# An FFT filter and MLP kernel: last FFT stage channel-major, residual by identity matmul, one-batch first units, loads paced

## The chip, the cores and the metric

The kernel runs on one core of one Trainium2 chip. The metric is the device time of one execution in microseconds (us). Before the change it was 720.28 us, the median of 3 runs (719.31 to 722.85). A run is "slow" when it is over 1.5% above the fastest of the same kernel. A "span" is the length of one profiled execution; it is about 2 us shorter than the device time.

Engines are called by the profile's names: PE is TensorE (matmul), PEld its weight loads, DVE VectorE, ACT ScalarE, POOL GpSimd and SP SyncE. "POOL queue" and "SP queue" mean the DMA transfers that those engines issue, in program order.

## The reference

```python
# x (8, 3136, 256); filt (1569, 256) complex; U (3136, 32); V (32, 3136)
X = np.fft.rfft(x, axis=1)
y = np.fft.irfft(X * F, n=3136, axis=1)          # a filter per channel
u = y + (y.transpose(0,2,1) @ U @ V).transpose(0,2,1)   # low-rank token mixing
out = u + np.maximum(u @ w_ch1, 0) @ w_ch2       # MLP 256 -> 1024 -> 256
```

## The kernel before

The length 3136 is split as 64 x 49. Batches are worked in units of two. For each unit:

1. **Stage 1 (`f1`)** multiplies x by a 64-point DFT and stores the result to DRAM (`ct1`), to be reloaded with another partition layout (`a2`).
2. **Middle stage (`mid`)**: for each of 33 frequencies a 49-point DFT (`pz`), the product with the filter on VectorE (`uv`), the inverse 49-point DFT (`pe`), an eviction on ScalarE, and a store to DRAM (`ct2`).
3. **Reload** (`load_e2`), then the low-rank product (`low_rank`, 25 multiplies that sum over all tokens).
4. **Groups** of 512 tokens: `stage4` (last FFT stage plus the low-rank term) makes u; transposes make it channel-major; `mm1` and `mm2` are the MLP.

The MLP of unit n fills TensorE while the middle stage of unit n+1 and stage 1 of unit n+2 are dealt out between its steps (8 steps per group) by a plan. Only the first unit has no MLP to hide behind.

```python
UNITS = [[0, 1], [2, 3], [4, 5], [6, 7]]

def f1(u):
    for c in range(6):
        asb = sb.tile([128, 4, bd], F16, tag="asb", bufs=2)
        for half in range(2):
            pf = ps.tile([128, 2, 512], F32, tag="w", bufs=1, name="pf")
            for i in range(nb):
                for h in range(2):
                    nc.tensor.matmul(pf[64*h:64*h+64, i, :], wf1[64*i:64*i+64, :],
                                     u.x[c][64*i:64*i+64, h, 2*half:2*half+2, :], ...)
            # evict: VectorE for one half, ScalarE for the other
            yield
        for h in range(2):
            nc.gpsimd.dma_start(dram(u.ct1, ...), asb[64*h:64*h+64])   # POOL queue
# ... cut

def stage4(gr):
    # four 64x64 multiplies by s2 (columns: two halves of the array), then
    # four with vsb as weights and u.h1 (low-rank result) streamed: u token-major
    gr.u16 = sb.tile([128, 2, 512], F16, tag="u", bufs=4, name="u16")
    nc.scalar.copy(gr.u16, pu)

def transposes(gr):
    # eight 128x128 transposes of u16 into pt (fp16), then
    nc.vector.tensor_copy(gr.ut[:, :, 0:gr.ntok], pt[:, :, 0:gr.ntok])

# end of mm2: nc.vector.tensor_add(dst, gv, uv)     adds u16 as the residual

# start
drain(f1(units[0])); load_x(units[1]); u_hat()
m0, fa = mid(units[0]), f1(units[1])
for i in range(34):                       # middle stage of unit 0, stage 1 of unit 1
    next(m0, None)
    if i >= 10 and i % 2 == 0:
        next(fa, None)
load_e2(units[0]); low_rank(units[0]); stage4(groups[0]); stage4(groups[1]); ...
# plan, per unit of `steps` steps (104 for 13 groups):
gens.append((mid(units[u.n + 1]), 34, 0, steps - 32))
gens.append((f1(units[u.n + 2]), 13, 0, steps))
# reload at step steps-31, low-rank product at steps-18, stage4 two groups ahead
```

## Time and profile before

| reading | value | view |
|---|---|---|
| first MLP multiply | 217.0 us | timeline |
| from there to the end | 500 us of a 717 us span | timeline |
| one 512-token group, late | 8.3 us | timeline |
| middle stage, first unit, per frequency | 2.1 to 2.2 us | timeline |

First, the page's rows of busy tenths. The span is cut into 40 slices of 17.9 us, a digit is the busy share of that slice in tenths, and PEclk is the granted clock.

```profile
PE   0000126766789999998999999999999999999996
DVE  0001125655553356621566654246665512122221
PEclk9999999999999999999999999999999999999999
DMA  9996567777673354578646351953343184230233
```

There are two regimes: TensorE has next to nothing to do in the first four slices and is full from the thirteenth on. In the first three the DMA engines are full. Next, the view of busy time by stretch: the window, its length, then busy us and instruction count of PE, PEld, DVE, ACT and POOL, then granted clock, DMA share and GB/s.

```profile
60.00:80.00 20.00, 2.76 (x20) 0.67 (x20) 3.67 (x3) 4.26 (x5) 4.99 (x8) 1.00 0.53 106
160.00:200.00 40.00, 28.57 (x64) 10.55 (x63) 22.66 (x20) 10.53 (x18) 11.19 (x17) 1.00 0.73 164
240.00:280.00 40.00, 39.84 (x278) 23.66 (x277) 20.67 (x22) 28.34 (x47) 8.42 (x13) 1.00 0.53 133
640.00:680.00 40.00, 40.00 (x301) 25.74 (x299) 9.68 (x14) 27.52 (x44) 0.00 (x0) 1.00 0.23 62
```

From 60 to 80 us every engine is busy for a quarter of the time at most and DMA for half: that stretch waits on latency. From 160 to 200 us PE shows 28.6 of 40, but with only 64 instructions. The view of waits says what the early stretch waits for (total us, times, longest):

```profile
DVE asb L224 <- DMA ct_0<-asb: 72.0, 5, 42.9
```

A stage-1 eviction needs its staging tile back. There are two such tiles, and U lies in one of them until stage 1 is over, so every tile waits for the store of the one before it. The first store was ready at 20.4 us (end of its eviction), but the POOL queue issued it at 50.15, behind the filter and weight loads: that wait took 42.9 us. The other four, 7.3 us each, are the plain round trip of a store; 72 us in five waits. In the middle stage the timeline (start, duration, engine, line, operation; in brackets the idle time before it and what ended it) shows a chain:

```profile
160.27 0.58 ACT L266 CAST esb<-pe 98x512 f16<-98x512 f32 x1 [1.52 <-PE pe L257]
160.90 0.59 PE L279 MATMUL pz<-a_384,tf_87 98*98 98x512 f16 x1 [0.67 <-ACT esb L266]
161.28 1.06 PE L257 MATMUL pe<-uv,g_89 98*98 98x512 f16 x2
161.53 1.22 DVE L286 TENSOR_TENSOR uv<-pz,fab 98x1024 f16<-98x1024 f32 x1 [0.89 <-PE pz L279]
162.42 0.58 ACT L266 CAST esb<-pe 98x512 f16<-98x512 f32 x1 [1.57 <-PE pe L257]
163.06 0.58 PE L279 MATMUL pz<-a_384,tf_87 98*98 98x512 f16 x1 [0.72 <-ACT esb L266]
```

`pz` and `pe` take turns in two PSUM buffers, so every next `pz` waits for ScalarE's eviction of `pe`: 163.06 − 160.90 = 2.16 us per frequency. Last, TensorE's timeline in a late group:

```profile
660.46 0.61 PE L371 MATMUL pt<-idn,u_6273 128*128 128x128 f16 x8
...
665.33 0.41 PE L350 MATMUL pu<-e_5383,s_91 64*64 64x512 f16 x4
665.68 0.61 PE L356 MATMUL pu<-h_5575,vsb 128*128 128x512 f16 x2
...
668.76 0.61 PE L371 MATMUL pt<-idn,u_6369 128*128 128x128 f16 x8
```

The transposes repeat after 668.76 − 660.46 = 8.30 us, and TensorE never waits between. The eight take 0.45 us (0.056 us from one start to the next). The four 64 x 64 multiplies of stage 4 take 0.35 us to the next multiply's start. Four of 512 columns one after the other would take 4 x 0.216 us. That is the overlap of small multiplies on different rows and columns of the array which the Trainium skill describes ("TensorE: Matmul & The Clock Gate", Part 3); this trace agrees.

### The profile page before, as it was taken

What the parts mean: (1) busy time and instruction counts of PE and PEld (TensorE: products, weight loads), DVE (VectorE), ACT (ScalarE), POOL (GpSimd) and SP (SyncE); (2) the same over time, 40 slices, a digit from 0 to 9 for tenths busy, and PEclk for the clock granted to TensorE, in tenths of its full rate; (3) what the DMA queues carried; (4) which work ended last, traced back from release to release, by engine and by line L of the source; (5) the groups of instructions that cost most, each with busy time, mean ns of one, the idle gap of its engine ahead of it and who ended that gap; (6) DMA issues with size and microseconds to landing.
All of it is one profiled execution on the core that took longest, in us unless ns stands there. A gap on an engine that the chain in (4) does not pass through costs nothing.

```text
span 716.9 us, 9884 instructions
## 1 busy us (share of the span) xinstructions
PE 581.4 (81%) x3797; PEld 330.4 (46%) x3797; DVE 288.1 (40%) x311; ACT 383.7 (54%) x634; POOL 126.8 (18%) x197
## 2 busy tenths in 40 slices
PE   0000126766789999998999999999999999999996
PEld 0000002222225656654565555565666665566664
DVE  0001125655553356621566654246665512122221
ACT  0004112432237676765767677567677765766663
POOL 3541342334111121211111111001111100000000
PEclk9999999999999999999999999999999999999999
DMA  9996567777673354578646351953343184230233
GB/s 189 172 181 137 117 130 213 189 166 155 158 203 71 82 150 131 132 193 218 190 119 196 88 150 44 283 162 115 103 126 108 54 183 129 63 88 15 76 89 95
DMA packets 47086, 97.88 MB, mean 137 GB/s; under 512 B 9336, under 2 KB 18108, under 8 KB 46942
## 3 DMA queue, kind: packets, MB, share of 16 engines
q0 software_dynamic: 27056, 43.93, 30.0%
q1 hardware_dynamic: 19984, 53.34, 27.3%
q8 instruction: 29, 0.48, 0.3%
q14 instruction: 17, 0.14, 0.1%
HBM read 64.05 MB, written 51.38 MB: 161 GB/s over the span
## 4 chain that ended last, share of the span: by engine, by line
PE 70%; DMA 13%; ACT 6%; issue 5%; POOL 2%; DVE 2%; SPq 1%; ACTq 0%; DVEq 0%; POOLq 0%
PE phh L379 22%; PE pc L415 21%; PE pe L257 10%; PE pz L279 5%; DMA ct_0<-asb 3%; PE pu L356 3%; PE pt L371 3%; ACT esb L266 3%; DMA x_75<-in_x_dram 3%; PE pu L350 2%; DMA fab<-in_filt_r_dram 2%; PE pf L214 2%; DMA e_2022<-ct_1 2%; ACT asb L222 2%; DMA fab<-in_filt_i_dram 2%
## 5 line engine op out<-in xcount | busy, mean ns | idle before, releaser
L379 PE MATMUL phh<-ut,w1sb 128*128 128x512 f16 (+1 forms) x832 | 237.6, 367 | 1.4 <-ACT h_2242 L382 0.2
L286 DVE TENSOR_TENSOR uv<-pz,fab 98x1024 f16<-98x1024 f32 x132 | 160.8, 1222 | 91.5 <-PE pz L279 91.2
L266 ACT CAST esb<-pe 98x512 f16<-98x512 f32 x128 | 74.6, 586 | 104.3 <-PE pe L257 103.3
L257 PE MATMUL pe<-uv,g_89 98*98 98x512 f16 x264 | 98.0, 462 | 3.0 <-DVE uv L286 2.0
L379 PEld LDWEIGHTS <-w1sb 128*128 128x128 f16 x832 | 78.6, 98 | 39.8 <-issue 12.6
L224 DVE CAST asb<-pf 128x1024 f16<-128x1024 f32 x24 | 29.3, 1222 | 97.0 <-DMA ct_0<-asb 72.0
L257 PEld LDWEIGHTS <-g_89 98*98 98x98 f16 x264 | 37.2, 144 | 54.3 <-issue 45.6
L214 PEld LDWEIGHTS <-wf_64 64*64 64x64 f16 x192 | 7.0, 114 | 118.8 <-issue 112.8
L222 ACT CAST asb<-pf 128x1024 f16<-128x1024 f32 x24 | 24.3, 1013 | 62.2 <-PE pf L214 60.5
L373 DVE COPY ut<-pt 128x1024 f16<-128x1024 f16 (+1 forms) x52 | 34.2, 657 | 15.2 <-PE pt L371 12.7
L214 PE MATMUL pf<-x_69,wf_64 64*64 64x512 f16 x8 | 1.3, 619 | 42.8 <-DVE asb L224 41.7
L279 PEld LDWEIGHTS <-tf_87 98*98 98x98 f16 x132 | 19.6, 148 | 17.3 <-issue 15.4
L268 POOL DMA_DIRECT2D ct_3<-esb x16 | 11.4, 710 | 90.2 <-ACT esb L266 83.6
L185 ACT COPY vsb<-vnat 128x768 f16<-128x768 f16 x4 | 7.0, 1829 | 34.6 <-DMA vnat<-in_moe_V_dram 34.6
L268 POOL DMA_DIRECT2D ct_1<-esb x16 | 11.5, 721 | 74.6 <-ACT esb L266 69.0
L268 POOL DMA_DIRECT2D ct_2<-esb x16 | 11.5, 720 | 63.5 <-ACT esb L266 50.4
L268 POOL DMA_DIRECT2D ct_0<-esb x16 | 11.9, 744 | 39.1 <-ACT esb L266 39.1
L214 PE MATMUL pf<-x_66,wf_64 64*64 64x512 f16 x8 | 1.9, 612 | 17.4 <-DMA x_66<-in_x_dram 16.1
L350 PEld LDWEIGHTS <-s_91 64*64 64x64 f16 x192 | 6.5, 103 | 19.4 <-issue 18.8
L227 POOL DMA_DIRECT2D ct_3<-asb x12 | 7.7, 648 | 27.2 <-ACT asb L222 27.2
L356 PEld LDWEIGHTS <-vsb 128*128 128x128 f16 x96 | 5.8, 97 | 11.1 <-issue 10.8
L227 POOL DMA_DIRECT2D ct_1<-asb x12 | 7.6, 640 | 12.5 <-ACT asb L222 12.5
(1605 smaller groups left out, 1235.7 us busy)
## 6 DMA issues: line engine op xcount, KB each, us to landing
out_dram<-och SPq DMA_DIRECT2D x128, 192.0 KB
ct_0<-esb POOLq DMA_DIRECT2D x16, 196.0 KB, 3.2
ct_1<-esb POOLq DMA_DIRECT2D x16, 196.0 KB, 3.5
ct_2<-esb POOLq DMA_DIRECT2D x16, 196.0 KB, 2.8
ct_3<-esb POOLq DMA_DIRECT2D x16, 196.0 KB, 2.8
ct_0<-asb POOLq DMA_DIRECT2D x12, 256.0 KB, 4.4
ct_1<-asb POOLq DMA_DIRECT2D x12, 256.0 KB, 4.2
ct_2<-asb POOLq DMA_DIRECT2D x12, 256.0 KB, 5.6
```

The costliest lines, as they stand in the source:

```text
L214: nc.tensor.matmul(pf[64 * h:64 * h + 64, i, :], wf1[64 * i:64 * i + 64, :], u.x[c][64 * i:64 * i + 64, h, 2 * half:2 * half + 2, :], star ...
L222: nc.scalar.copy(dst, src)
L224: nc.vector.tensor_copy(dst, src)
L257: nc.tensor.matmul(pe[0:98, 0:bd], g3[:, (2 * k + l) * 98:(2 * k + l + 1) * 98], uv[:, l * bd:(l + 1) * bd], start=(k != 32 and l == 0), s ...
L266: nc.scalar.copy(st["esb"][:, slot % 2, :], pe[0:98, 0:bd])
L268: nc.gpsimd.dma_start(dram(u.ct2, (slot - 1) * 98 * bd, [[bd, 98], [98 * bd, 2], [1, bd]]), st["esb"])
L279: nc.tensor.matmul(pz[0:98, 0:bd], tf2[:, k * 98:(k + 1) * 98], a2[slot // 4][:, slot % 4, :], start=True, stop=True)
L286: nc.vector.tensor_mul(uv.rearrange("p (f b d) -> p f b d", f=2, b=nb), zin, fin)
L356: nc.tensor.matmul(pu[:, h, jj * bd:(jj + 1) * bd], vsb[:, v0:v0 + 128], u.h1, start=False, stop=True, skip_group_check=True)
L373: nc.vector.tensor_copy(gr.ut[:, :, 0:gr.ntok], pt[:, :, 0:gr.ntok])
L379: nc.tensor.matmul(ph[:, 0:n], w1sb[:, dh * 1024 + t * 128:dh * 1024 + (t + 1) * 128], gr.ut[:, dh, 0:n], start=(dh == 0), stop=(dh == 1))
L415: nc.tensor.matmul(gr.pc[:, col * DM:(col + 1) * DM], gr.h[tt][:, i * 128:(i + 1) * 128], w2sb[:, tt * DM:(tt + 1) * DM], start=(tt == 0), ...
```

## The change

Its intent: make u channel-major directly in the last FFT stage, by using the reloaded tile as weights and `s2` as the moving operand. The transposes and one ScalarE cast go; the residual u is then added inside PSUM by an identity multiply. Stage 1 becomes one block-diagonal multiply over 128 rows. The first two units have one batch each, so that the MLP can start earlier; the filters are read once and mirrored in SBUF, the first unit's stage-1 stores go to the SP queue, U leaves stage 1's staging tiles, and x is loaded two tiles ahead.

```diff
-UNITS = [[0, 1], [2, 3], [4, 5], [6, 7]]
+UNITS = [[0], [1], [2, 3], [4, 5], [6, 7]]
 # wf1 and s2 become block-diagonal 128x128 (cut)
 # filters: loaded once into fab[:, 0], in two parts, then mirrored (cut)
+    def mirror_filters(a, z):
+        nc.sync.dma_start(fab[0:NR, 1, a:z, :], fab[NR:98, 0, a:z, :])
+        nc.sync.dma_start(fab[NR:98, 1, a:z, :], fab[0:NR, 0, a:z, :])
 # f1
+        eng = nc.sync if u.n == 0 else nc.gpsimd
+            if load_ahead and c + load_ahead <= nx:
+                load_x(u, c + load_ahead)
+                    nc.tensor.matmul(pf[:, i, :], wf1, u.x[c][:, r:r + 2, :], ...)
 # stage4: e2 and h1 as weights, s2 and vsb streamed
+            for i in range(4):
+                nc.tensor.matmul(pu[:, dh, i * 128:(i + 1) * 128],
+                                 e2[:, y, j % cj + jj, d0:d0 + 128], s2, ...)
+                nc.tensor.matmul(po[:, b], u.h1[:, d0:d0 + 128], vv[...], ...)
-        gr.u16 = sb.tile([128, 2, 512], F16, tag="u", bufs=4, name="u16")
-        nc.scalar.copy(gr.u16, pu)
-    def transposes(gr): ...
+        nc.vector.tensor_copy(gr.ut, pu)
 # residual, at the end of mm2
+                nc.tensor.matmul(o[:, dh*128:dh*128+128], gr.ut[:, dh, t0:t0 + n], idn,
+                                 start=False, stop=(dh == 1), skip_group_check=True)
-            nc.vector.tensor_add(dst, gv, uv)
+            nc.vector.tensor_copy(dst, gr.pc.rearrange(...))
 # plan over all 53 groups; first[n] is the first step of unit n
+    mids = [mid(units[0], "o")] + [mid(u) for u in units[1:]]
+    deal(f1s[1], 7, 0, 6)
+    deal(mids[1], 34, 9, 35)
+    for u in units[2:]:
+        z = first[u.n] - 22
+        a = first[u.n - 1]
+        if u.n == 2:
+            deal(f1s[2], 13, 14, a + 8)
+            deal(mids[2], 34, a + 10, z)
+        else:
+            deal(f1s[u.n], 13, first[u.n - 2] + 28, a - 4)
+            deal(mids[u.n], 34, a, z)
-                stage4(groups[n + 2])
+                stage4(groups[n + 1])
-                if step == 8 * (u.ng + 1) - 31:
+                if step == first[u.n + 1] - 20:
                     load_e2(units[u.n + 1])
-                if step == 8 * (u.ng + 1) - 18:
+                if step == first[u.n + 1] - 10:
                     low_rank(units[u.n + 1])
```

The middle stage of the next unit now ends 22 steps before that unit instead of 32, its reload is issued at −20 instead of −31, and its low-rank product comes at −10 instead of −18. A late step is about 1.04 us (8.3 us in 8 steps).

## The prediction

> **What bounds it now.** Two regimes. By the busy-time-by-stretch view TensorE is 93 to 100% busy in every stretch from 200 to 680 us; the first MLP multiply starts at 217.0 us (timeline). Before that, latency and DMA bind: TensorE works 5.3 of the first 80 us. First-stage stores sit on the GpSimd queue behind all loads (one eviction waits 42.9 us), then stage 1 goes at a store round trip (8.5 us) per tile until 98 us; the middle stage runs 111 to 212 us at 2.13 us per frequency, chained pz, pe, ScalarE eviction, next pz. There 512-column matmuls start 0.43 us apart, later 0.22: the half-rate clock that the Trainium skill ("TensorE: Matmul & The Clock Gate", Part 1) gives for a sparse array. The trace agrees, though the granted-clock row says 1.0.
>
> **Saturated part.** One 512-token group takes 8.3 us (timeline at 660 us): mm1 3.46, mm2 3.49, stage 4 0.88, transposes 0.45.
> - Removed: 8 transposes (56 ns each); a ScalarE cast (1.01 us); the fp16 eviction 0.69.
> - Added: 8 identity multiplies with weight loads, 0.45 us; VectorE evicts u from fp32, 1.22. Output adds become copies, about 0.69.
> - Stage 4 becomes 8 x 128 plus 4 x 256 columns, about 0.88 us.
> - Block-diagonal stage 1: four 64-row multiplies already overlap pairwise (four in 0.64 us, tail included); two full ones cost the same.
> TensorE work per group is unchanged to about 0.1 us. ScalarE loses 1.0 us, VectorE gains 0.5; neither bounds there. Channel-major u alone buys nearly nothing.
>
> **The gain: start-up.** One-batch units halve what must precede the MLP: x 1.6 MB (as stored) instead of 3.2, filters read once and mirrored, stores on another queue. Estimates from the rates above (about 180 GB/s):
> - x landed about 18 us, stage 1 stored 28, filters mirrored and middle stage started 36.
> - Middle stage at half width: product 0.69 us, pz 0.40 cold, so about 1.3 us per frequency, 44 us, plus 7 us of V copies (4 x 1.83) in ScalarE's queue: done about 88.
> - Store, reload, low rank, stage 4: first MLP multiply about 107 us, 110 us earlier.
>
> **Given back.** Work formerly in start-up moves into the saturated part. TensorE sums there (from the instruction order, 0.216 us per 512 columns): before 476 us, measured 500; after about 506: middle stage 75 instead of 55, stage 1 17 instead of 10, an extra 64-token group 2. With the same 24 us excess: 530. Also, units 1 and 2 pack 10 to 13 frequencies per group; there VectorE (1.22 us each plus 2.6 per group) and the single-buffered pz chain (0.38 + 1.22 + 0.1 us) exceed TensorE: about +10 us. Stage 4 is only one group ahead and the low-rank product closer to its reload: about +8 us over four unit boundaries. 107 + 548 = 655 us span; minus a few for reordering, plus 3 outside the span.
>
> **Predicted: 652 us, 80% range 628 to 676.** Faster by over 2%: 0.97; within: 0.02; slower: 0.01.
>
> **Right if:** first MLP multiply at 95 to 120 us; unit 0's middle stage at about 1.3 us per frequency; late groups 8.2 to 8.4 us; TensorE busy near 88% of the span; gaps at unit boundaries and in units 0 and 1. Wrong if late groups change by over 0.2 us, or the MLP starts outside that window.
>
> **What would make it wrong.** Weight loads of the 128-column multiplies not hidden; filters or mirrors landing after 45 us; V copies blocking ScalarE on a late V; reloads stalling each boundary over 5 us; or the early middle stages fitting without stalls (about 635).

## The result, and the profile after

The changed kernel took 698.87 us (median of 4 runs, 696.35 to 700.45) against 719.79 (4 runs, 718.11 to 722.85). The ratio is 0.9701, 95% interval 0.9656 to 0.9746. A ratio here is the mean time of one kernel's fast runs over that of the other's of the same rounds, so it is not quite the ratio of the medians that are quoted. The change is faster by 3.0%, where 9.5% had been predicted; 698.87 lies well above the range of 628 to 676.

The page's rows of the changed kernel (slices of 17.4 us):

```profile
PE   1203446999888998748999999989999998999995
DVE  0104342477424897213766664247665622232231
PEclk9999556999989999967999999999999999999999
DMA  8994443869676487892255725952524286031133
```

TensorE is full from the eighth slice instead of the thirteenth. But it sags in slices 11 to 13 and again, down to 7, 4 and 8, in slices 17 to 19, and there the clock row drops as well. VectorE shows 8, 9, 7 just ahead of that second sag. By stretch:

```profile
100.00:120.00 20.00, 10.04 (x55) 4.29 (x56) 2.45 (x2) 3.71 (x7) 1.88 (x3) 0.56 0.42 91
240.00:280.00 40.00, 37.26 (x220) 21.31 (x218) 33.31 (x31) 24.80 (x43) 15.53 (x23) 1.00 0.76 186
280.00:320.00 40.00, 24.74 (x169) 14.40 (x168) 6.96 (x9) 10.38 (x22) 9.44 (x16) 0.78 0.82 225
640.00:680.00 40.00, 40.00 (x327) 28.53 (x325) 11.64 (x15) 22.98 (x39) 0.00 (x0) 1.00 0.30 79
```

From 240 to 280 us VectorE is 83% busy, and from 280 to 320 TensorE shows 24.7 of 40 at 0.78 of its clock. Late in the kernel nothing changed, as TensorE's timeline there says (compare the late group of before):

```profile
643.57 0.28 PE L425 MATMUL pc<-idn,ut 128*128 128x128 f16 x2
...
644.12 0.39 PE L394 MATMUL pu<-s_79,e_5887 128*128 128x128 f16 x4
644.34 0.38 PE L400 MATMUL pu<-vsb,h_6037 128*128 128x256 f16 x2
...
652.39 0.39 PE L394 MATMUL pu<-s_79,e_5890 128*128 128x128 f16 x4
```

Stage 4 returns after 652.39 − 644.12 = 8.27 us. The eight identity multiplies (L425) cost what the eight transposes cost, and stage 4, now of 128-column multiplies with their own weight loads (four in 0.22 us, 0.055 each), costs about what it cost before.

The sag at 300 us in TensorE's timeline is the reload at the boundary from the second unit to the third:

```profile
301.35 0.27 PE L425 MATMUL pc<-idn,ut 128*64 128x128 f16 x2
305.35 0.51 PE L350 MATMUL ph<-e_2460,ut_121 128*32 128x512 f16 x3 [3.73 <-DMA e_2460<-ct_2]
311.10 0.61 PE L350 MATMUL ph<-e_2463,ut_121 128*32 128x512 f16 x3 [5.25 <-DMA e_2463<-ct_2]
```

The chain of work that ended last (start, length, what) passes through the same transfer:

```profile
293.27 17.79 DMA e_2463<-ct_2
311.10 1.89 PE ph L350 x15
```

TensorE's waits (total us, times, longest) put that in proportion:

```profile
PE pz L315 <- DMA a_169<-ct_0: 22.0, 1, 22.0
...
PE pe L290 <- ACT esb L299: 11.2, 5, 8.4
PE pz L315 <- DVE uv L322: 10.3, 5, 9.0
PE ph L350 <- DMA e_499<-ct_0: 9.4, 1, 9.4
...
PE ph L350 <- DMA e_2463<-ct_2: 5.2, 1, 5.2
PE ph L350 <- DMA e_1366<-ct_1: 5.0, 1, 5.0
```

The first four belong, for the most part, to the start, before the MLP. The visible waits after it are few and short, which is why the next step needs a sum and not this list.

### Where the time went: a sum of the streamed columns

The busy time of PE is not its work. The Trainium skill says ("Perfetto Trace Analysis", Identifying the Most-Contended Engine) that matmul busy time is not a good measure of how close TensorE is to its limit, because matmuls are pipelined. Here it shows too much: in 240 to 280 us of the changed kernel the view shows 37.3 us of PE busy, but its multiplies, counted at the spacing that they have in a full group, add up to 34.4 us; in 280 to 320 us it shows 24.7 and the sum is 16.6. So each multiply after the first MLP multiply was counted at its spacing in saturated groups (rounded: 0.216 us per 512 columns, 0.108 per 256, 0.056 per 128; those on a quarter of the array at half, those of 32 output columns at a quarter, because they overlap). "Lost" is the rest of the time from the first MLP multiply to the end. This sum is an own calculation from the traces, in us:

```
kernel   MLP starts   columns after   lost   span
before     217.0         472.5          27   716.9
after      114.1         503.6          79   696.5
```

The start gained 103 us. Work moved behind it cost 31. The remaining 52 us were newly lost, leaving 20. By unit (from one unit's first MLP multiply to the next's):

```
before   unit starts 217.0 344.6 478.6 607.3        lost  8.1  4.7  4.7 10.0
after    unit starts 114.1 205.2 317.1 456.1 586.8  lost 21.2 32.2  9.6  6.6  9.2
```

The first two batches were through at 344.6 us before and at 317.1 after. The two one-batch units lose 53 us where the one two-batch unit that they replace loses 8. Within the second of them, the gaps in TensorE's stream stand in front of the low-rank product (12.2 us), the middle stage (8.2), stage 1 (4.3), mm1 (2.9), stage 4 (2.5) and mm2 (1.4).

Four explanations were put to the test; the expectations quoted below may name them in other words. *Crowding*: the one-batch units have too few groups (7 each) to carry the next unit's stage 1, middle stage and reload. *VectorE*: the fp32 eviction of u loads VectorE where it is already full. *Channel-major u*: the new stage 4 costs a little in every group. *Spacing*: the plan puts middle stage, reload and low-rank product closer together. A separate question was how much of the earlier start the one-batch units are needed for, since the change also moved the stores off the blocked queue.

### The profile page after: what moved, and what is told of

The parts are those of the page before. It is cut to its first block, busy times and chain, and to the rows that moved or that the text cites. A ratio compares the mean times of both kernels' runs of the same rounds, so it can differ in the third digit from the quotient of the medians.

```text
span 696.5 us, 10531 instructions
## 1 busy us (share of the span) xinstructions
PE 574.6 (83%) x4128; PEld 379.2 (54%) x4128; DVE 314.7 (45%) x343; ACT 342.9 (49%) x627; POOL 138.4 (20%) x216
## 4 chain that ended last, share of the span: by engine, by line
PE 63%; DMA 11%; ACT 5%; issue 4%; POOL 3%; DVE 1%; SPq 1%; ACTq 0%; POOLq 0%
PE phh L409 21%; PE pc L453 20%; PE pe L290 6%; PE pz L315 4%; PE pu L400 3%; PE pu L394 3%; PE pc L425 3%; DMA e_2463<-ct_2 3%; DMA ct_2<-esb 2%; DMA e_1366<-ct_1 1%; PE pf L243 1%; SPq L336 1%; DMA ct_1<-esb 1%; PE ph L350 1%; DMA e_502<-ct_0 1%
## 5 line engine op out<-in xcount | busy, mean ns | idle before, releaser
L409 PE MATMUL phh<-ut,w1sb 128*128 128x512 f16 (+2 forms) x848 | 244.6, 369 | 6.1 <-DVE ut L403 3.9
L322 DVE TENSOR_TENSOR uv<-pz,fab 98x1024 f16<-98x1024 f32 (+1 forms) x165 | 163.0, 1008 | 102.6 <-PE pz L315 56.3
L299 ACT CAST esb<-pe 98x512 f16<-98x512 f32 (+1 forms) x160 | 79.3, 501 | 107.1 <-PE pe L290 90.5
L463 DVE COPY och<-pc 128x512 f32<-128x512 f32 x96 | 66.2, 689 | 108.0 <-PE pc L425 107.4
L403 DVE CAST ut<-pu 128x1024 f16<-128x1024 f32 x48 | 58.8, 1224 | 111.8 <-PE pu L400 111.7
L290 PE MATMUL pe<-uv,g_81 98*98 98x512 f16 (+1 forms) x330 | 89.8, 363 | 11.3 <-ACT esb L299 11.2
L290 PEld LDWEIGHTS <-g_81 98*98 98x98 f16 x330 | 44.8, 138 | 41.6 <-issue 28.2
L425 PE MATMUL pc<-idn,ut 128*128 128x128 f16 (+1 forms) x394 | 55.1, 221 | 0.0
L243 PE MATMUL pf<-x,wf_64 128*128 128x512 f16 x96 | 32.3, 412 | 25.1 <-DMA x<-in_x_dram 13.9
L425 PEld LDWEIGHTS <-ut 128*128 128x128 f16 (+1 forms) x394 | 38.6, 99 | 5.9 <-issue 0.2
L148 POOL DMA_DIRECT2D x<-in_x_dram x48 | 26.5, 560 | 35.2 <-PE pf L243 29.8
```

Source lines behind the costliest of these rows:

```text
L243: nc.tensor.matmul(pf[:, i, :], wf1, u.x[c][:, r:r + 2, :], start=True, stop=True)
L290: nc.tensor.matmul(pe[0:98, 0:bd], g3[:, (2 * k + l) * 98:(2 * k + l + 1) * 98], uv[:, l * bd:(l + 1) * bd], start=(k != 32 and l == 0), s ...
L299: nc.scalar.copy(st["esb"][:, slot % 2, :], pe[0:98, 0:bd])
L322: nc.vector.tensor_mul(uv.rearrange("p (f b d) -> p f b d", f=2, b=nb), zin, fin)
L403: nc.vector.tensor_copy(gr.ut, pu)
L409: nc.tensor.matmul(ph[:, 0:n], w1sb[:, dh * 1024 + t * 128:dh * 1024 + (t + 1) * 128], gr.ut[:, dh, 0:n], start=(dh == 0), stop=(dh == 1))
```

## The experiments

All 13 kernels gave correct results. For each, "before" is the kernel before in the same rounds.

### e1: stage 1 of the fourth unit dealt later

```diff
-            deal(f1s[u.n], 13, first[u.n - 2] + 28, a - 4)
-            deal(mids[u.n], 34, a, z)
+            late = u.n == 3
+            deal(f1s[u.n], 13, a if late else first[u.n - 2] + 28, a + 26 if late else a - 4)
+            deal(mids[u.n], 34, a + 30 if late else a, z)
```

> The changed kernel, with the first FFT stage of batches 4 and 5 (and its loads of x) moved from the MLP of the second one-batch unit into the MLP of the two-batch unit after it. Theory A (the middle stages, first stages and reloads of the next unit do not fit under a one-batch MLP: they crowd DMA and VectorE there): TensorE's loss before the low-rank product at the end of the second unit, 12.2 us, falls to about 5, the 4.3 us lost before first-stage multiplies goes, the second unit's MLP shrinks from 112 us to about 97, the next one grows by 5 us; whole 688 to 691 us instead of 699. Rival B (the loss is the chain of the middle stage itself and the reload's own length, whatever runs beside it): only the 5 us of first-stage work moves, whole 697 to 701 us.

Measured: 702.85 us (before 719.29), ratio 0.9769 [0.9717, 0.9821]. The second unit, relieved of that work, took 96 us instead of 112, as hoped; but the third took 160 instead of 139, with gaps in front of the middle stage (6.7 us), the low-rank product (4.6) and stage 1 (2.9), among others. The total loss was 84 instead of 79. The device time is above both forecasts, but its interval overlaps that of the change, so the times don't tell the two apart. Moving work out of the crowded unit only moved the crowding.

### e2: the eviction of u on ScalarE in the one-batch units

```diff
-        nc.vector.tensor_copy(gr.ut, pu)
+        (nc.scalar.copy if u.n < 2 else nc.vector.tensor_copy)(gr.ut, pu)
```

> The changed kernel, with the eviction of u (1.22 us on VectorE per group) given to ScalarE in the two one-batch units. If VectorE's load sets the pace of the middle stages there, as the prediction said, TensorE's loss before middle-stage multiplies (5.4 and 8.2 us) falls by half or more and the whole by 5 to 8 us, to 691 to 694 us. If the reloads and the DMA set it, the whole stays within 2 us of 699.

Measured: 694.1 us (before 719.29), ratio 0.9656 [0.963, 0.9682]; the loss went from 79 to 71. VectorE is part of the loss, but worth only about 5 us of device time (8 us of loss in the profiled executions, of which 1 came back as a later start); the interval overlaps that of the change (0.9656 to 0.9746), so this pair alone is at the edge of what can be told apart. e9 settles it below.

### e3: channel-major u alone, in the kernel before

```diff
 # before, with block-diagonal s2, the changed order of V, stage4 and output rows,
 # no transposes, ut bufs=4, still two groups ahead
+        nc.vector.tensor_copy(gr.ut, pu)
+        if half:
+            residual(gr, o, i * 128, 128)
-            nc.vector.tensor_add(dst, gv, uv)
+            nc.vector.tensor_copy(dst, gr.pc.rearrange(...))
```

> The kernel before, with the channel-major last FFT stage and the identity-matmul residual alone (units, start-up, first stage and loads as before). The prediction's step: TensorE work per group is unchanged, so late groups stay at 8.2 to 8.4 us and the whole is within 1% of before, 713 to 725 us. Rival: the removed pass through ScalarE, or the fp32 evictions that VectorE gains, move the whole by over 1%.

Measured: 716.33 us (before 719.29), ratio 0.9951 [0.9924, 0.9979]. The late groups take 8.3 us. So channel-major u is not the cause: it costs nothing and gains about half a per cent.

### e4: the first unit's stage-1 stores moved to the SP queue, and U out of stage 1's tiles, in the kernel before

The matrix U was staged in one of the two `asb` buffers; it moves to a free one so that stage 1 doesn't wait for it.

```diff
-    usb = sb.tile([64, NR * RANK], F16, tag="asb", bufs=2)
+    usb = sb.tile([64, NR * RANK], F16, tag="e2", bufs=5, name="usb")
+        eng = nc.sync if u.n == 0 else nc.gpsimd
-                nc.gpsimd.dma_start(
+                eng.dma_start(
```

> The kernel before, with only the stores of the first unit's first FFT stage moved to the Sync queue and U's staging tile moved out of the two buffers that this stage uses. If queue order and buffers, not the size of the first unit, made the slow start: stage 1 of unit 0 ends near 58 us instead of 98, the MLP starts near 172 us instead of 217, the later part is unchanged (500 us), whole 660 to 690 us, as fast as the whole change or faster. If the loads themselves bound the start, the gain is under 20 us: 700 us or more.

Measured: 696.35 us (before 719.29), ratio 0.9671 [0.9647, 0.9696], which is not told apart from the whole change's 0.9701 [0.9656, 0.9746]. The timeline shows the last multiply of stage 1 and the first of the middle stage:

```profile
50.82 0.42 PE L234 MATMUL pf<-xl,wf 64*64 64x256 f16 x2 [1.15 <-ACT asb L223]
...
72.54 1.01 PE L280 MATMUL pz<-a,tf 98*98 98x512 f16 x2 [21.30 <-DMA a<-ct]
```

Stage 1 ends at 51 us instead of 98, and the middle stage starts at 72.5 instead of 111. The MLP starts at 196.9 instead of 217.0, and all of those 20 us arrive at the end: the loss behind it is 27 us as before. What was gained at the MLP's start, with no work moved behind it, was kept. But the forecast (MLP near 172 us, 660 to 690 us in all) was missed: of the 48 us won at the end of stage 1, 28 were lost again before the MLP, in a middle stage that took longer (first product to last 84 us instead of 69) and behind it; why was not followed up. Nor were the two edits run apart. Read from the trace of before, and not tested, the queue made most of the wait of 42.9 us, and the tile that U held made the four of 7.3.

### e5: the change with two-batch units

Everything of the change stays except the one-batch units; stage 1 of the second unit is interleaved in the start, as in the kernel before.

```diff
-UNITS = [[0], [1], [2, 3], [4, 5], [6, 7]]
+UNITS = [[0, 1], [2, 3], [4, 5], [6, 7]]
+        if i >= 10 and i % 2 == 0:
+            next(f1s[1])
 # plan: deal(mids[u.n], 34, a, z) for every unit from the second on
```

> The changed kernel with its one part 'one-batch first units' undone: four units of two batches; channel-major last stage, block-diagonal stage 1, filters read once, stores of the first unit on the Sync queue, the plan's rules as in the change. Theory A (the stalls come from putting a two-batch middle stage and its reload under a one-batch MLP): the MLP starts later, near 150 us instead of 114, but TensorE's loss after it falls from 79 us to 35 us or less, so the whole is 650 to 675 us, faster than the change. Rival C (the stalls come from the other parts, such as VectorE's longer eviction or the last stage prepared only one group ahead): the loss stays near 79 us and the whole is 700 us or more.

Measured: 690.44 us (before 719.86), ratio 0.9585 [0.9549, 0.9621]: faster than the change itself, and the intervals don't touch. The MLP starts at 167.6 us, 53 us later than in the change, but the loss is 39 instead of 79 and the columns behind it are 21 us fewer. This is the test of crowding, and it holds, though not to the forecast size (MLP near 150 us, 35 us of loss or less, 650 to 675 us in all): the one-batch units pay for their 53 us of earlier start with 61 us (40 of loss, 21 of columns). In device time they cost some 8 us on balance.

### e6 and e7: loads that are not needed at once, held back until stage 1 is done

V and the MLP weights, in e7 the next unit's x as well, get a one-column copy from stage 1's last tile written into their tiles first, so that their loads can't start sooner (in e6, x only stands behind them in the program). e6 does this to e5 (and loads the second half of the filters later), e7 to the change.

```diff
+    def late_loads():
+        for t in (vnat[0:64, 0:1], vnat[64:128, 0:1], w1sb[0:64, 0:1], w2sb[0:64, 0:1]):
+            nc.vector.tensor_copy(t, units[0].al[0:64, 0:1])
+        # then the loads of V, w1, w2 as before
```

> The same, with the loads that the start does not need yet (V, both MLP weights, x of the next unit) held back until the first unit's first stage is done, and the second half of the filters behind the first unit's last x. If DMA bandwidth binds the start, the middle stage starts some 10 us earlier and so does the MLP: 10 us under the two-batch kernel without it. If not, within 3 us of it.

> The changed kernel with V, both MLP weights and the second unit's x held back until the first unit's first stage is done. If DMA crowding made the middle stage start at 60 us where the prediction had 36, it starts near 47 us now and the MLP near 101 us instead of 114; the later part keeps its 582 us: 684 to 689 us. If the earlier start is lost again in the crowded one-batch units: 695 to 700 us.

Measured: e6 691.9 us, ratio 0.9597 [0.9544, 0.965]; e7 696.19 us, ratio 0.9665 [0.9619, 0.971] (before 719.86). Neither is told apart from the kernel it was made from (0.9585 and 0.9701). In e7 the gate opened at 31 us, before the later of the two mirrors that the first product reads was issued (44.8) and used (61.6), so the loads still ran beside it. It is no test of whether they delay them; e8 is.

### e8 and e9: the same loads held back until the middle stage runs; e9 with the edit of e2 as well

```diff
+            if u.n == 0 and pos == 3:
+                late_loads(uv)          # gate: the product of the fourth frequency
```

> The changed kernel again with V, both MLP weights and the second unit's x held back, this time until the fourth product of the first unit's middle stage exists (the earlier try let them go at 31 us, while the stores, reloads and filter mirrors were still waiting for DMA). Some 3.4 MB at about 200 GB/s are out of the way: if they delayed the start, the first product comes near 47 us instead of 60 and the MLP starts near 101 us instead of 114; the rest unchanged: 684 to 689 us. If the mirrors and reloads are slow by themselves: no change, 695 to 700 us.

> The same, with the eviction of u on ScalarE in the one-batch units (worth 5 us by itself). If the two causes are separate, they add: 679 to 684 us. If the earlier start is lost in the crowded units, no better than 690 us.

Measured: e8 692.8 us, ratio 0.9626 [0.9594, 0.9658]; e9 687.03 us, ratio 0.9536 [0.9491, 0.9582] (before 720.13). The first filter product of e8 came at 43.8 us instead of 60.5, so the held-back loads had indeed been in the way: of stage 1's stores (the reload that waits for them was issued at 36.9 us instead of 43.3) and of the mirrors (from the issue of the later one to the first product 5.6 us instead of 15.8). The profile names the mirror as what that product waited for, in the first line below. But the MLP started only 5 us earlier (108.6), and the times fell between the forecasts. The timeline shows why:

```profile
43.82 3.12 DVE L330 TENSOR_TENSOR uv<-pz,fab 98x512 f16<-98x512 f32 x5 [16.27 <-DMA fab<-fab]
...
62.76 0.76 POOL L309 DMA_DIRECT2D ct<-esb  x1 [5.62 <-DMA w1sb<-in_moe_w_ch_dram]
...
73.24 0.65 ACT L307 CAST esb<-pe 98x256 f16<-98x256 f32 x2 [9.80 <-DMA ct<-esb]
74.29 2.00 DVE L330 TENSOR_TENSOR uv<-pz,fab 98x512 f16<-98x512 f32 x3 [21.48 <-PE pe L298]
```

The late loads stand in the POOL queue ahead of the middle stage's own stores; the stores come late, ScalarE waits 9.8 us for their tiles, and VectorE has nothing for 21.5 us. (Part of that is the V copies on ScalarE, which the change has too; its gap there is 9.8 us.) Of the 16.7 us won at the first product, 11 were given back in the same stage. e9 adds e2's edit and gains another 5.8 us on e8, with intervals that don't touch: relieving VectorE is worth its 5 us here too, so the two effects are about additive. (The intervals of e8 and the change just touch.)

### e10 and e11: the two-batch version with late loads, and with the spacing of before

e10 is e6 with the later gate of e8. e11 is e10 with the three numbers of the plan put back to those of the kernel before:

```diff
-        z = first[u.n] - 22
+        z = first[u.n] - 32
-                if step == first[u.n + 1] - 20:
+                if step == first[u.n + 1] - 31:
-                if step == first[u.n + 1] - 10:
+                if step == first[u.n + 1] - 18:
```

> Four two-batch units with the change's other parts, and the loads held back until the fourth product. If DMA crowding binds the start here too: the MLP starts near 155 us instead of 167, whole near 678 us. If not, 688 to 692 us.

> The same, with the spacing of the kernel before: a middle stage ends 32 steps before the next unit instead of 22, its reload starts 31 steps before instead of 20, the low-rank product runs 18 steps before instead of 10. If the reload's exposed time is what the plan's spacing costs, TensorE's loss before the low-rank product at the first boundary falls from 6 us to 3 and the whole by 3 to 6 us against the same kernel without it; if not, the same within 2 us.

Measured: e10 692.75 us, ratio 0.9617 [0.9593, 0.964], no gain over e5. e11 674.89 us (672.65 to 677.13; before 720.13), ratio 0.9383 [0.9354, 0.9412]. The three numbers alone are worth 18 us, where 3 to 6 had been forecast, and the loss falls from 38 to 20 us, below that of the kernel before. In the first unit of e10 15.2 us were lost, 6.9 of them in front of the low-rank product; in e11 3.9. The view by stretch, first for e10, then for e11 (columns as above):

```profile
280.00:320.00 40.00, 31.27 (x245) 19.89 (x243) 7.62 (x10) 16.78 (x34) 3.62 (x6) 0.91 0.82 208
```

```profile
280.00:320.00 40.00, 39.28 (x313) 25.81 (x311) 19.27 (x21) 22.77 (x44) 5.05 (x8) 1.00 0.67 199
```

So the spacing is a cause as well, and in the two-batch form a large one. Spaced out, TensorE is full across the boundary. e11 also clears a suspect of the prediction: it prepares stage 4 only one group ahead, as the change does, and yet loses less than the kernel before, which prepares it two ahead.

### e12: the old spacing in the change, where its units are long enough

```diff
-        z = first[u.n] - 22
+        z = first[u.n] - (32 if u.n > 2 else 22)
 # and the reload at -31, the low-rank product at -18, for u.n > 1 only
```

> The changed kernel with the spacing of the kernel before (middle stage ends 32 steps before the next unit, reload 31, low rank 18) at the two boundaries between two-batch units alone; the one-batch units are too short for it. If the spacing, not only the short units, cost time: TensorE's loss in the third and fourth unit falls from 9.6 and 6.6 us to about 4 each and the whole by 6 to 9 us, to 690 to 693 us; the one-batch units keep their loss of 53 us. If the spacing does not matter with one-batch units: 697 to 701 us.

Measured: 692.98 us (before 718.41), ratio 0.9649 [0.9623, 0.9675]. The interval overlaps that of the change, so the times alone don't separate them. The units in the trace do: the third and fourth lose 6.0 and 4.6 us instead of 9.6 and 6.6, while the one-batch units lose 20.9 and 33.4, unchanged. The spacing explains about 6 us of the change's loss, at the later boundaries. At the first two it was not tried, for a unit of 7 groups has only 56 steps.

### e13: e11 with the second unit's stage 1 moved behind the MLP's start

```diff
-        if i >= 10 and i % 2 == 0:
-            next(f1s[1])
+            deal(f1s[1], 13, 0, 22)
+            deal(mids[1], 34, 26, z)
```

> The two-batch kernel with spacing and late loads, and the second unit's first stage, with its x, moved out of the start into the first unit's MLP (its middle stage after it). If bytes bound the start (x, stores and reloads of the second unit are some 9.6 MB of about 33, at about 200 GB/s), the MLP starts near 132 us instead of 168, at a cost of 5 us of TensorE work and a few us of stalls later: 638 to 652 us. If latency chains bound it, the MLP starts after 155 us and the whole stays over 665 us.

Measured: 674.79 us (674.32 to 676.76; before 718.41), ratio 0.939 [0.9374, 0.9406]: a tie with e11. The MLP started 21 us earlier (146.6), the columns behind it rose by 6 us and the loss from 20 to 40; the first unit alone lost 22.9, of which 10.6 in front of the middle stage. Again an earlier start was handed back in full. (The MLP had been forecast near 132 us if bytes bound the start, after 155 if latency did: it fell between.)

The sums of all kernels, calculated as above (us):

```
kernel   MLP starts   columns after   lost   span
e1         115.4         503.7          84   703.0
e2         115.2         503.9          71   690.0
e3         218.1         473.5          23   714.6
e4         196.9         472.5          27   696.4
e5         167.6         482.8          39   689.4
e6         166.5         482.6          39   688.4
e7         113.2         503.7          78   694.6
e8         108.6         503.8          82   694.2
e9         109.8         503.7          73   686.1
e10        168.2         482.7          38   689.1
e11        168.0         482.6          20   670.9
e12        114.4         503.9          73   691.7
e13        146.6         488.5          40   675.0
```

The best versions are e11 and e13, 675 us, 6% below the kernel before and 3.4% below the change.

## Why the prediction was wrong

**What held.**

- *The saturated group is unchanged.* Predicted 8.2 to 8.4 us, measured 8.3; e3, which is that part alone, gave 0.9951. "Channel-major u alone buys nearly nothing" is what it showed.
- *The start.* Predicted 107 us for the first MLP multiply, window 95 to 120; measured 114.1. The 7 us came through two wrong terms that nearly cancelled. The filters were predicted at 36 us and the first product came at 60.5. The middle stage, predicted at 1.3 us per frequency, then ran at about 0.64 between its stops, and took 36 us (60.5 to 96.6), V copies included, where 52 (36 to 88) had been predicted: 24 us late, 16 us regained there and 1.5 behind it (17.5 us to the MLP instead of 19). That the sum fell into the window is luck. The trace of the changed kernel shows the wait and the speed (the mirror's issue, the first multiply of the stage, twelve products in 7.56 us, and the V copies):

```profile
44.62 0.75 SPq L180 DMA_DIRECT2D fab<-fab  x1
51.63 0.59 PE L315 MATMUL pz<-a_169,tf_77 98*98 98x256 f16 x2 [22.02 <-DMA a_169<-ct_0]
60.46 7.56 DVE L322 TENSOR_TENSOR uv<-pz,fab 98x512 f16<-98x512 f32 x12 [33.42 <-DMA x<-in_x_dram]
69.67 7.02 ACT L208 COPY vsb<-vnat 128x768 f16<-128x768 f16 x4
77.24 1.01 PE L290 MATMUL pe<-uv,g_81 98*98 98x256 f16 x4 [8.44 <-ACT esb L299]
```

  Different PSUM tags let `pz` and `pe` each have two buffers in the first unit, so the chain of before was gone, and VectorE did one product after the other; the prediction still added up the parts of a chain. (No run changed the tags alone.) The four V copies block ScalarE for 7.0 us in one piece, as predicted. The bracket at 60.46 names the x load that the profile saw last; the product reads the mirrored filters, and that it was they which it waited for is what e8's trace says. They were late twice: the one of 44.62 stood in the SP queue behind the stage's first reloads (issued from 43.3 us), and then took long.
- *The work moved behind the start.* Predicted +30 us of columns (476 to 506), measured +31 (472.5 to 503.6).

**What failed** is the step "Given back", above all its term "about +10 us" for the packed early units; the others are the usual "24 us excess" and "about +8 us over four unit boundaries". That is 42 us of loss in all; the trace has 79. These 37 us and the 7 at the start, less 2 for columns (503.6 instead of 506), are the 42 us by which the changed kernel's span (696.5) exceeds the prediction's sum (107 + 548 = 655).

The step had the right list and wrong sizes. It counted the units' work on each engine and added what exceeded TensorE's time. It foresaw 10 to 13 frequencies per group, and the trace has up to 13. What came out too small is what this costs: 53 us were lost in the two one-batch units, boundaries included, where 8 had been lost before, so 45 more in place of 10 and a part of the 8. The gaps in front of the low-rank product alone, where the reload ends, are 5.5 and 12.2 us in these units. In the second, three groups of 15 to 19 us carry 8 to 11 frequencies each; then the last part of the reload took 17.8 us, with little but one 64-token group behind which to hide. The two later boundaries cost 7 us more than before (16 against 9). The runs bound the parts: undoing only the one-batch units (e5) takes the loss to 39. VectorE's share is about 8 us (the loss of e2 against that of the change); the spacing at the later boundaries is about 6 (e12); the last unit's 9 us were there before. TensorE's clock adds to it: the trace records half clock from 70.0 to 117.8 us, and behind the MLP's start from 192.9 to 199.7, 295.3 to 298.7 and 305.5 to 322.6; a pair of mm1's 512-column multiplies takes 1.01 us at 114 us, against 0.59 late (0.43 and 0.22 us from start to start). The Trainium skill ("TensorE: Matmul & The Clock Gate", Part 1) says that the array is slowed after an idle window of about 3.4 us and restored after about 3.4 us of activity; the stretch at 305.5 begins after TensorE stood idle for 3.7 us up to 305.35 (the timeline above), which fits. An estimate from these records: multiplies worth 11 us at full spacing started in the slow stretches after 114.1 us, so half clock cost at most about 11 of the 79 us. No run tested it.

**What the prediction didn't ask** is whether the one-batch units were the source of the gain at all. e4 gets 20 us of earlier start from the stores' queue and U's tile, as much as the whole change gains in the end, and e11 starts 49 us earlier and keeps 46 of them (span 670.9 against 716.9). The chance given to "faster by over 2%" was right, the size was not.

**What stays open.** Where e4 lost 28 of the 48 us that it won in stage 1 is not known. How the 53 us of the one-batch units divide among reload, the `pz` chain, VectorE and half clock was not measured apart; the waits overlap, and e1 and e8 show that removing one moves the loss elsewhere. What sets the two-batch start of 167 us was bounded only in part: neither order nor gating moved it (e6, e10), and taking the second unit's x and stage-1 traffic out of it moved it by 21 us (e13). A version that keeps e13's start and not its 20 us of new loss was not found.

## What to carry to other kernels

Starting the saturated part earlier pays only what the work behind the start can hide: e1, e8 and e13 each freed one stretch and saw the next one give it back, while e4 started the MLP 20 us earlier without adding work behind it and kept all 20. When a pipeline is made finer at its head, check that each short stage still has room between the store, the reload and the first use; three numbers of that spacing were worth 18 us here, nearly the gain of the whole change. And measure a saturated engine by the columns it streamed, not by its busy time, before sizing what is lost.

## What the Trainium skill lacked or had wrong

- "Trainium Kernel Development and Optimization", Key Constraints, says that issuing DMAs from several engines "only saves the sequencer's issue time". In e4, moving the first unit's stores from the POOL queue to the SP queue (and U out of a stage-1 tile, which may have its part) started the MLP 20 us earlier and took 23 us off the time. In the kernel before, a store that was ready at 20.4 us was issued by the POOL queue at 50.15, behind the loads, and one eviction waited 42.9 us for it. The sentence may hold for bandwidth, but this section says nothing of such a wait.
- The same section has nothing on the reverse: in e8, loads held back on purpose stood ahead of the middle stage's stores in the same POOL queue; ScalarE waited 9.8 us for the tiles, and VectorE was idle for 21.5 us, V copies included (9.8 us in the change).
- "TensorE: Matmul & The Clock Gate", Part 1, warns that clock events in a trace can't always be trusted, but not of this: the granted-clock row of this profile shows 1.0 until the first clock record, which came at 212.7 us in the kernel before, although two 512-column multiplies stood 0.43 us apart there and 0.22 us later. Before the first record the clock has to be judged by the spacing of equal multiplies.
- "DMA: Bandwidth & Descriptors" gives no time for an SBUF-to-SBUF copy among other loads. The later mirror of the first filters, issued at 44.6 us in the changed kernel, was first used at 60.5 us, 15.8 us later; with the other loads held back (e8) it was issued at 38.2 and used at 43.8, 5.6 us later.
